# Feed-forward units moved to an earlier attention job: finer first groups of weight blocks, one converted block per job

## The chip, the cores and the metric

The kernel runs on one core of one Trainium2 chip. The metric is the device time of one execution in microseconds; less is better. The kernel before took 1116.96 us (median of three runs, 1116.5 to 1118.39).

## The reference

Two layers, one after the other. Attention with decay, 8 batches of 8 heads, 576 positions, 64 values per head:

```
scores = scale * np.matmul(q, k.transpose(0, 1, 3, 2))
log_f = np.log(np.clip(f, 0.0001, 1.0))
cum = np.cumsum(log_f, axis=-1)
decay = cum[:, :, :, None] - cum[:, :, None, :]
scores = np.where(causal, -1000000000.0, scores + decay)
...
attn = attn / (np.sum(attn, axis=-1, keepdims=True) + 1e-09)
return np.matmul(attn, v).astype(np.float32)
```

Then a feed-forward layer on the 4608 tokens of 512 values, with `w_in` of 512 x 2048 and `w_out` of 2048 x 512:

```
h = x @ w_in
g = np.where(pos, h, np.where(neg, 0.0, (h + beta) ** 2 / (4.0 * beta)))
return (g @ w_out).astype(np.float32)
```

## The kernel before

**Attention in jobs.** A job is one pair of heads of one batch. The four pairs of batch 0 are cut by rows (`CUTS`): jobs 0 to 3 do row tiles 0 and 1 (256 positions), jobs 4 to 7 tiles 2 to 4. From job 8 on a job does all five tiles (four of 128 rows, one of 64, which holds both heads) of a pair; there are 36 jobs. For a row tile, PE multiplies queries and keys into a PSUM tile `s` (`scores`, L482), of which there are two. Meanwhile POOL computes the decay scores into an `sdr` tile (L488) and masks it (L492). In `weights` DVE adds the two and takes each row's extremum in one instruction (L571, which leaves it in `nm`; below "the maximum"); ACT takes the exponential and the row sum (L575). What follows depends on the job: in jobs 0 to 4 the normalised weights are turned by PE against a diagonal (`turn_rows`: ACT makes the diagonal from the identity, L502, PE multiplies, L513, "the turning products", and ACT copies into `pT`, L524). From job 5 on they are split into two float16 halves, `pr` (ACT L589, DVE L595; for some tiles of jobs 6 and 7 POOL does the second, L593), and SP's DMA transposes them (L601, L604). The `sdr` tiles are a ring: POOL may write one again only when the job before has read it.

A job's products with the values come in the middle of the job after it (`finish`). With the last pair of a row part they make tokens of the feed-forward layer available: 256 tokens, which is chunk 0, at `finish` of job 3, that is in job 4, and 512 at `finish` of job 7.

**Weights.** The feed-forward weights are 8 blocks of 256 hidden units. A block comes as two loads (`w_in` part, `w_out` part), in words that `weight_split` turns into floats: three integer passes on DVE per load (L211, L214, L217), a sum of squares on ACT (L221), from it a scale, then a high half on ACT (L225) and a low half: on POOL for `w_in` (L227, L228), on DVE for `w_out` (L230). `CONVERT` says how many blocks are converted in which job: before, block 0 in job 1, block 1 in job 2, blocks 2 and 3 in job 3, block 4 in job 5, block 5 in job 6, the others in jobs 9 and 10.

**Feed-forward units.** A unit is one chunk of 256 tokens with one block. `moe_front` multiplies tokens and `w_in` (L657, 24 products into a tile `ph`), and ACT and DVE make the activation and its two halves `g` (L666, L667, L668, L670, L671). `moe_back`, called two units later, multiplies `g` with `w_out` (L685, 12 "output products") into a pair of PSUM tiles `po`, of which there is one pair. While not all blocks are converted, the blocks of a chunk go in groups (`EARLY`): each group has scales of its own (`moe_scales`, 17 small DVE instructions, L289 to L314), and at its end `po` is evicted: the first group of a chunk by an ACT copy into `ot` (L702), a later one by a DVE multiply and add (L698).

**The order.** `EARLY` is also the order of the first units. In each job, `ready()` counts the units whose tokens are there, and a quota of them is spread over the steps that are left in the batch. It is taken ahead of a job's steps, so job 4, in whose middle chunk 0 becomes available, has a quota of 0; jobs 5 to 8 did 2, 2, 1 and 1 units. A scheduler then sets the final order on each engine from the program; every engine works through its own list strictly in order, SP its DMA issues too.

Of the kernel before, what the change touches and what calls it, by code (L numbers as in the profile page):

```python
# [8 lines left out]
F32 = mybir.dt.float32  # L9
F16 = mybir.dt.float16  # L10
I32 = mybir.dt.int32
AF = mybir.ActivationFunctionType
ALU = mybir.AluOpType
AX = mybir.AxisListType

P = 128
EVEN_EXP = 0x7F000000
HALF_BIAS = 0x1FC00000
# [14 lines left out]

POOL_LOW = {6: (2, 4), 7: (2, 4)}

EARLY = ((0, 0, 4), (0, 4, 6), (1, 0, 4), (1, 4, 6), (0, 6, 8), (1, 6, 8))

CONVERT = {1: 1, 2: 1, 3: 2, 5: 1, 6: 1, 9: 1, 10: 2}
LOADS = {0: 3, 1: 6, 2: 8}
AHEAD = 4  # L40

# [4 lines left out]
def kernel(  # L46
# [19 lines left out]
    nc = tc.nc  # L66
# [3 lines left out]
    NPAIR = H // 2  # L70
    NT5 = -(-S // P)
# [5 lines left out]
    NB = NF // 2  # L77
# [6 lines left out]
    const = ctx.enter_context(tc.tile_pool(name="const", bufs=1))  # L84
# [3 lines left out]
    tiny = ctx.enter_context(tc.tile_pool(name="tiny", bufs=4))  # L88
# [94 lines left out]
    sw = const.tile([P, 2, NB], F32, name="sw")  # L183
# [53 lines left out]
    sv = const.tile([P, B], F32, name="sv")  # L237
# [22 lines left out]
    def value_step(b, i):  # L260

        if 0 < i <= NPAIR:
            value_max(b, i - 1)
        if i < NPAIR:
            value_load(b, i)

    def value_scale(b):
        m1 = tiny.tile([P, 1], F32, name="m1", bufs=2)
        nc.vector.tensor_reduce(out=m1, in_=vmax[b], axis=AX.X, op=ALU.max)
        m = mv[:, b:b + 1]  # L270
        across(m, m1)
        if b:
            nc.vector.tensor_tensor(out=m, in0=m, in1=mv[:, b - 1:b], op=ALU.max)
        scale_of(sv[:, b:b + 1], pv[:, b:b + 1], m)

    early_z = const.tile([P, 5, NB], F32, name="early_z")

    class Scales:
        pass

    def moe_scales(b, first=0, last=NB - 1, early_group=False):

        z = Scales()
        z.first, z.last = first, last
        blocks = slice(first, last + 1)
        n = last + 1 - first
        w = early_z[:, :, blocks] if early_group else tiny.tile([P, 5, NB], F32, name="z")
        z.t, z.h, z.u, z.r, z.o = (w[:, i] for i in range(5))
        nc.vector.tensor_scalar(out=z.t, in0=sw[:, 0, blocks], scalar1=sv[:, b:b + 1], scalar2=None, op0=ALU.mult)  # L289
        nc.vector.tensor_scalar(  # L290
            out=z.h.bitcast(I32), in0=z.t.bitcast(I32), scalar1=1, scalar2=None, op0=ALU.logical_shift_right
        )
        nc.vector.tensor_scalar(
            out=z.h.bitcast(I32), in0=z.h.bitcast(I32), scalar1=HALF_BIAS, scalar2=None, op0=ALU.add
        )
        nc.vector.reciprocal(z.u, z.h)
        nc.vector.tensor_scalar(out=z.u, in0=z.u, scalar1=0.5, scalar2=None, op0=ALU.mult)
        nc.vector.tensor_scalar(out=z.h, in0=z.h, scalar1=0.5, scalar2=None, op0=ALU.mult)
        gm = tiny.tile([P, 1], F32, name="gm", bufs=2)
        sm = tiny.tile([P, 1], F32, name="sm", bufs=2)  # L300
        nc.vector.tensor_reduce(out=gm, in_=mp[:, 0, blocks], axis=AX.X, op=ALU.max)
        nc.vector.tensor_reduce(out=sm, in_=mp[:, 1, blocks], axis=AX.X, op=ALU.max)
        nc.vector.tensor_scalar(
            out=gm, in0=gm, scalar1=mv[:, b:b + 1], scalar2=OVER * 1.001 * DM ** 0.5, op0=ALU.mult, op1=ALU.mult
        )
        nc.vector.tensor_scalar(out=gm, in0=gm, scalar1=1.0, scalar2=None, op0=ALU.max)
        even_pow2(gm, gm)
        z.osc = z.o[:, 0:1]
        nc.vector.tensor_scalar(
            out=z.osc, in0=gm, scalar1=sm, scalar2=4.0 / PSC, op0=ALU.mult, op1=ALU.mult  # L310
        )
        nc.vector.tensor_tensor(out=z.r, in0=z.t, in1=sw[:, 1, blocks], op=ALU.mult)
        nc.vector.tensor_scalar(out=z.r, in0=z.r, scalar1=z.osc, scalar2=None, op0=ALU.mult)
        nc.vector.reciprocal(z.r, z.r)  # L314
        return z
# [43 lines left out]
    def load_decay(w, h):  # L359
        bh = w.b * H + 2 * w.hp + h  # L360
        ck = two.tile([P, S], F32, name="ck", bufs=3)
        nc.sync.dma_start(
            ck[:, 0:w.s1], cum_d[bh:bh + 1, 0:w.s1].broadcast_to([P, w.s1])
        )
        w.ck.append(ck)
# [43 lines left out]
    def prepare(w):  # L409
        if w.p < NQK:  # L410
            return early_prepare(w)
        sc = w.sc
        for j in range(2):
            nc.scalar.activation(qs[:, 2 * j], w.x32[j], AF.Copy, scale=sc[:, j:j + 1])  # L414
        for j in range(2):
            nc.vector.scalar_tensor_tensor(  # L416
                out=qs[:, 2 * j + 1], in0=w.x32[j], scalar=sc[:, j:j + 1], in1=qs[:, 2 * j],
                op0=ALU.mult, op1=ALU.subtract,
            )
        qkT = two.tile([P, 4, SP], F16, name="qkT")  # L420
        nc.sync.dma_start_transpose(
            qkT.rearrange("p c (b e) -> p (c b) e", e=P), qs.rearrange("p c e -> p (c e)")
        )
        qh, ql, kh, kl = (qkT[:, c] for c in range(4))
        w.terms = ((qh, kh), (ql, kh), (qh, kl))
# [288 lines left out]

    units = [(ch, fb) for ch, first, end in EARLY for fb in range(first, end)]
    units += [(ch, fb) for ch in range(NCH) if ch not in [e[0] for e in EARLY] for fb in range(NB)]
    groups = sorted({e[1:] for e in EARLY})
    done = 0
    tokens = 0
    nload = 0  # L720
# [14 lines left out]
    def weight_step():  # L735
# [25 lines left out]
    for p in range(njobs + 1):  # L761
        w = pairs[p] if p < njobs else None
        nxt = pairs[p + 1] if p + 1 < njobs else None
        steps = []
        if w:
            if w.b not in xs:
                xs[w.b] = xpool.tile([P, NPAIR, 2, S], F16, name="x")
            if nxt:
                load_decay(nxt, 0)
                prepare(nxt)  # L770
            scores(w, w.r0)

            def step(r):
                if r + 1 < w.r1:
                    scores(w, r + 1)
                if r == w.r1 - 2 and nxt:
                    load_decay(nxt, 1)
                    split_values(nxt)
                weights(w, r)
                if r == w.r0 and p + 3 < njobs:  # L780
                    pairs.append(load(p + 3))
                if w.r1 == NT5 and w.b + 1 < B:
                    n = w.r1 - w.r0
                    i = w.hp * n + r - w.r0 - (NPAIR - 1) * n + -(-(NPAIR + 1) // n) * n
                    if 0 <= i <= NPAIR:
                        value_step(w.b + 1, i)
                    if w.hp == NPAIR - 1 and r == w.r0:
                        value_scale(w.b + 1)
                if r == w.r1 - 1 and p + 2 < njobs:
                    measure(pairs[p + 2])  # L790

            steps = [lambda r=r: step(r) for r in range(w.r0, w.r1)]
        if p > 0:
            wp = pairs[p - 1]

            def finish():
                nonlocal tokens
                (early_values if wp.p < NPE else values)(wp, xs[wp.b])
                if wp.hp == NPAIR - 1:
                    if wp.b and wp.r0 == 0:  # L800
                        join_scales(wp.b - 1)
                    tokens = wp.b * S + wp.s1

            steps.insert(4 if len(steps) == NT5 else 2, finish)
        load_weights(LOADS.get(p, 0))
        blocks = CONVERT.get(p, 0)
        quota = -(-ready() // (NPAIR - (p + NPAIR - 1) % NPAIR))
        before, converted = done, 0
        for i, st in enumerate(steps):
            st()  # L810
            while converted < blocks * (i + 1) // len(steps):
                weight_step()
                converted += 1
            while ready() and done - before < quota * (i + 1) // len(steps):
                if units[done] not in bsc and nw < 2 * NB:
                    break
                moe_unit(*units[done])
                done += 1
# [35 lines left out]
```

## Time and profile before

| | |
|---|---|
| median of three runs | 1116.96 us |
| the profiled execution | 1118.56 us |
| its span | 1116.8 us |
| mean granted PE clock | 0.966 |
| PE, DVE, ACT, POOL busy in the span | 91%, 72%, 71%, 38% |
| PE busy in 60 to 290 us | 167.05 of 230 us |
| DVE busy in 60 to 290 us | 186.47 of 230 us |

Engines: PE multiplies matrices (PEld loads its weights), DVE is the vector engine, ACT the activation engine, POOL is GpSimd, SP issues the DMAs. A row of the timeline has the start and the duration in us, the engine, the line of the kernel, the operation, what it writes and reads, a count, and in brackets how long the engine stood idle before it and whose work ended that. A group by line has count, then busy time and mean duration in ns of one, then the idle time before. The granted clock is the share of PE's full clock that it was given. In the profile's time, job 4's first maximum is at 68.21 us, job 5's at 90.88, job 6's at 111.56, job 7's at 131.19 and job 8's at 151.09.

### The profile page before, as it was taken

How to read it: one execution, taken by the hardware profiler on the slowest of the kernel's cores; microseconds unless marked ns; L12 is line 12 of the kernel's file. 1: busy time of each engine (PE TensorE's matmuls, PEld its weight loads, DVE VectorE, ACT ScalarE, POOL GpSimd, SP SyncE). 2: the span in 40 equal slices, each digit the busy share in tenths (PEclk: the TensorE clock that was granted, in tenths of full speed). 3: DMA queues.
4: the chain of work that ended last, by engine and by line, in shares of the span. 5: the costliest groups of instructions: out<-in, count | busy, mean ns of one | idle time of the engine just before them, and what ended most of it. 6: DMA issues, size and time to landing. Idle time of an engine off the chain costs nothing. (4 is left out here: it accounts for less than half of the span.)

```text
span 1116.8 us, 24410 instructions
## 1 busy us (share of the span) xinstructions
PE 1017.8 (91%) x8811; PEld 663.8 (59%) x8811; DVE 799.0 (72%) x2095; ACT 790.0 (71%) x1638; POOL 427.4 (38%) x679
## 2 busy tenths in 40 slices
PE   4647789667999999999999999999999999999998
PEld 3424455335566666666766666566666666677665
DVE  4785987887989888887667668888888787322222
ACT  3665887756877887788667768787878887444443
POOL 3486665634544543343223324344343442000000
PEclk9968889778999999999999999999999999999999
DMA  7957765575978657766653666775776462200000
GB/s 235 303 143 222 167 147 125 142 191 116 190 172 166 159 143 170 167 152 148 118 140 78 155 119 153 168 174 139 166 167 155 116 124 73 66 21 1 19 20 19
DMA packets 408281, 152.18 MB, mean 136 GB/s; under 512 B 383968, under 2 KB 384992, under 8 KB 408160
## 3 DMA queue, kind: packets, MB, share of 16 engines
q1 hardware_dynamic: 408160, 150.63, 57.6%
q8 instruction: 69, 1.13, 0.4%
q14 instruction: 52, 0.43, 0.1%
HBM read 75.64 MB, written 9.58 MB: 76 GB/s over the span
## 5 line engine op out<-in xcount | busy, mean ns | idle before, releaser
L657 PE MATMUL ph<-x,place 128*128 128x256 f16 (+3 forms) x4608 | 413.3, 248 | 6.4 <-DVE u L668 5.5
L685 PE MATMUL po<-place,g 128*128 128x512 f16 x1728 | 401.9, 382 | 12.4 <-ACT g L670 8.2
L657 PEld LDWEIGHTS <-place 128*128 128x128 f16 x4608 | 354.1, 99 | 66.3 <-issue 18.0
L685 PEld LDWEIGHTS <-g 128*128 128x128 f16 x1728 | 166.4, 99 | 192.0 <-ACT g L670 10.5
L488 POOL TENSOR_SCALAR sdr<-ck,nsig,cqs 128x128 f32<-128x128 f32 (+1 forms) x192 | 145.8, 763 | 149.2 <-DVE pr L595 137.3
L575 ACT ACTIVATE sdr<-sdr,nm 128x384 f32<-128x384 f32 (+1 forms) x248 | 137.4, 554 | 66.9 <-DVE nm L571 57.0
L668 DVE SCALAR_TENSOR_TENSOR u<-ph,z,u 128x512 f32<-128x512 f32 x128 | 95.8, 748 | 113.1 <-ACT u L667 112.5
L488 POOL TENSOR_SCALAR sd<-ck,nsig,cqs 64x576 f32<-64x576 f32 x48 | 60.0, 1250 | 248.7 <-ACT qs L414 109.3
L666 ACT ACTIVATE u<-ph,z 128x512 f32<-128x512 f32 x128 | 97.9, 765 | 78.4 <-PE ph L657 78.4
L482 PE MATMUL s<-qkT 64*64 64x512 f16 (+11 forms) x1056 | 119.6, 342 | 34.1 <-DVE nm L571 30.6
L595 DVE SCALAR_TENSOR_TENSOR pr<-sdr,rc,pr 128x384 f16<-128x384 f32 (+2 forms) x232 | 130.5, 596 | 21.6 <-ACT pr L589 20.4
L670 ACT ACTIVATE g<-u,z 128x512 f16<-128x512 f32 x128 | 91.9, 718 | 67.6 <-DVE u L668 67.3
L671 DVE SCALAR_TENSOR_TENSOR g<-u,z,g 128x512 f16<-128x512 f32 x128 | 96.7, 756 | 47.2 <-ACT g L670 46.5
L589 ACT ACTIVATE pr<-sdr,rc 128x384 f16<-128x384 f32 (+1 forms) x236 | 119.3, 556 | 12.1 <-DVE rc L586 5.3
L571 DVE CUSTOM_DVE_ANT_0 sdr<-s,sdr,nalpha 128x128 f32<-128x128 f32 (+1 forms) x192 | 99.0, 545 | 13.1 <-PE s L482 8.3
L492 POOL TENSOR_SCALAR_AFFINE_SELECT sdr<-sdr 128x128 f32<-128x128 f32 x248 | 93.9, 389 | 9.7
L667 ACT ACTIVATE u<-u 128x512 f32<-128x512 f32 x144 | 89.5, 622 | 2.0
L615 PE MATMUL s<-pT,vs 128*64 128x320 f16 (+3 forms) x1098 | 70.9, 282 | 4.7 <-DVE nm L571 4.7
L615 PEld LDWEIGHTS <-vs 128*64 128x64 f16 x1098 | 49.7, 112 | 27.3 <-issue 8.8
L488 POOL TENSOR_SCALAR sdr<-ck,cq 128x384 f32<-128x384 f32 (+3 forms) x56 | 39.9, 712 | 66.2 <-DVE pr L595 38.3
L482 PEld LDWEIGHTS <-qkT 64*128 64x128 f16 (+1 forms) x864 | 33.8, 99 | 51.3 <-issue 35.9
L414 ACT ACTIVATE qs<-qk,sc 128x640 f16<-128x640 f32 x48 | 37.0, 818 | 22.4 <-DVE sc L140 22.4
(154 smaller groups left out, 1013.8 us busy)
## 6 DMA issues: line engine op xcount, KB each, us to landing
ck<-cum_d SPq DMA_DIRECT2D x64, 288.0 KB, 3.8
out_dram<-ot SPq DMA_DIRECT2D x36, 256.0 KB, 2.1
qk<-in_k_dram SPq DMA_DIRECT2D x64, 128.0 KB, 2.7
vst<-in_v_dram SPq DMA_DIRECT2D x28, 288.0 KB, 3.3
v<-in_v_dram SPq DMA_DIRECT2D x62, 128.0 KB, 2.6
qk<-in_q_dram SPq DMA_DIRECT2D x56, 128.0 KB, 2.7
place<-in_moe_w_in_dram SPq DMA_DIRECT2D x6, 1024.0 KB, 7.2
place<-in_moe_w_out_dram SPq DMA_DIRECT2D x5, 1024.0 KB, 7.2
```

What stands on the lines that cost most here:

```text
L482: nc.tensor.matmul(sds[h % len(sds)][1][p0:p1, c0:c1], lhsT=a[rows, q0 - w.s0:q0 - w.s0 + p1 - p0], rhs=b[rows, c0:c1], start=(i == 0), st ...
L488: nc.gpsimd.tensor_scalar(out=sd[p0:p1, 0:wid], in0=w.ck[h][p0:p1, 0:wid], scalar1=w.nsig if w.p < NQK else w.nsig[p0:p1], scalar2=w.cqs[p ...
L571: nc.vector.tensor_tensor_reduce(out=a, in0=sp[:, 0:wid], in1=a, scale=w.nalpha, scalar=BIG, op0=ALU.add, op1=ALU.min, accum_out=nm[:, i:i ...
L575: nc.scalar.activation(a, a, AF.Exp, bias=nm[:, i:i + 1], scale=-1.0, accum_out=sm[:, i:i + 1])
L589: nc.scalar.activation(pr[:, :, 0, i, :], a, AF.Copy, scale=rc[:, i:i + 1])
L595: nc.vector.scalar_tensor_tensor(out=pr[:, :, 1, i, :], in0=a, scalar=rc[:, i:i + 1], in1=pr[:, :, 0, i, :], op0=ALU.mult, op1=ALU.subtract,)
L615: nc.tensor.matmul(av[64 * h:64 * h + 64, at + s0:at + s1], lhsT=w.vs[:, vl, h, t, :], rhs=w.pT[:, t, pl, h, s0:s1], start=(t == 0 and pi ...
L657: nc.tensor.matmul(ph[:, fi, a0:a1], lhsT=wi[fb][:, wl, t, fi * P:(fi + 1) * P], rhs=xs[b][:, t, xl, s0:s0 + a1 - a0], start=(fi == 0 and ...
L666: nc.scalar.activation(u, h, AF.Relu, scale=z.u[:, i:i + 1], bias=z.h[:, i:i + 1])
L668: nc.vector.scalar_tensor_tensor(out=u, in0=h, scalar=z.t[:, i:i + 1], in1=u, op0=ALU.max, op1=ALU.min)
L671: nc.vector.scalar_tensor_tensor(out=g[:, 1], in0=u, scalar=z.r[:, i:i + 1], in1=g[:, 0], op0=ALU.mult, op1=ALU.subtract)
L685: nc.tensor.matmul(po[ch][i], lhsT=g[:, gl, fi * TC + i * P:fi * TC + (i + 1) * P], rhs=wo[fb][:, wl, fi, :], start=(first and fi == 0 and ...
```

## The change

Chunk 0's first six blocks go in three groups of two; chunk 1's first six in one. Job 4 is put into a new table `FIRST`: `finish` comes ahead of its row tiles instead of among them, and directly behind it two units are done, (0, 0) and (0, 1); jobs 5 to 8 then have one each. Block 3 is converted in job 4 instead of job 3, so jobs 1 to 6 convert one block each. As groups now overlap (blocks 0 to 5 as one group for chunk 1, as three for chunk 0), the part of the scales that depends on a block alone is computed once for each block (`block_scales`), and each group has its own place for the rest.

```diff
-EARLY = ((0, 0, 4), (0, 4, 6), (1, 0, 4), (1, 4, 6), (0, 6, 8), (1, 6, 8))
+EARLY = ((0, 0, 2), (0, 2, 4), (0, 4, 6), (1, 0, 6), (0, 6, 8), (1, 6, 8))
+FIRST = {4: 2}
-CONVERT = {1: 1, 2: 1, 3: 2, 5: 1, 6: 1, 9: 1, 10: 2}
+CONVERT = {1: 1, 2: 1, 3: 1, 4: 1, 5: 1, 6: 1, 9: 1, 10: 2}
...
+        if early_group:
+            at = groups.index((first, last + 1))
+            z.t, z.h, z.u = (early_z[:, i * NB + first:i * NB + first + n] for i in range(3))
+            z.r = early_r[:, starts[at]:starts[at] + n]
+            z.osc = early_r[:, starts[-1] + at:starts[-1] + at + 1]
+            fresh = slice(made[0], last + 1)
+            if made[0] <= last:
+                block_scales(*(early_z[:, i * NB + made[0]:i * NB + last + 1] for i in range(3)), b, fresh)
+                made[0] = last + 1
...
-            steps.insert(4 if len(steps) == NT5 else 2, finish)
+            steps.insert(0 if p in FIRST else 4 if len(steps) == NT5 else 2, finish)
...
-        quota = -(-ready() // (NPAIR - (p + NPAIR - 1) % NPAIR))
+        quota = FIRST.get(p) or -(-ready() // (NPAIR - (p + NPAIR - 1) % NPAIR))
...
-            while ready() and done - before < quota * (i + 1) // len(steps):
+            while ready() and done - before < (quota if p in FIRST else quota * (i + 1) // len(steps)):
```

What this moves on three engines, as the order of the instructions has it (each row is one instruction, or several alike with their count; the line numbers of after are higher by 19 in most of the rows shown, and by 1 in `weight_split`).

POOL, before, between the last tile of job 4 and the first of job 5. `place` is the weight store, `ck` and `cq` are the decay sums; `sdr_101` and `sdr_102` are the scores of job 5's first tile, one for each head:

```order
L488 TENSOR_SCALAR sd_1_106<-ck,cq 64x576
L492 AFFINE_SELECT sd_1_106<-sd_1_106 64x64
L227 TENSOR_SCALAR place<-place,sw 128x1024
L228 TENSOR_TENSOR place<-place 128x1024
L227 TENSOR_SCALAR place<-place,sw 128x1024
L228 TENSOR_TENSOR place<-place 128x1024
L488 TENSOR_SCALAR sdr_101<-ck,cq 128x384
L488 TENSOR_SCALAR sdr_102<-ck,cq 128x384
```

And after:

```order
L228 TENSOR_SCALAR place<-place,sw 128x1024
L511 AFFINE_SELECT sd_1_106<-sd_1_106 64x64
L507 TENSOR_SCALAR sd_1_106<-ck,cq 64x576
L229 TENSOR_TENSOR place<-place 128x1024
L511 AFFINE_SELECT sd_1_106<-sd_1_106 64x64
L507 TENSOR_SCALAR sdr_101<-ck,cq 128x384
L507 TENSOR_SCALAR sdr_102<-ck,cq 128x384
```

Before, blocks 2 and 3 stand ahead of job 5's scores; after, block 2 alone.

PE, before, from the transposes of job 5's queries and keys to job 4's turning products (L513):

```order
L388 MATMUL s<-ident,qk_0_98 128x128 x4
L388 MATMUL s<-ident,qk_0_98 128x64
L131 MATMUL ph<-m2w,ones 128x2
L482 MATMUL s<-qkT 128x384 x2
L513 MATMUL ph<-pr_112,sdr_101 128x128 x2
L513 MATMUL ph<-pr_112,sdr_102 128x128
```

After, from the scores of job 4's last tile on; the 48 front products of the two units (L676) stand ahead of these rows:

```order
L501 MATMUL s<-qkT 64x512 x2
L501 MATMUL s<-qkT 64x64 x2
L407 MATMUL s<-ident,qk_0_98 128x128 x2
L407 MATMUL s<-ident,qk_0_98 128x64
L407 MATMUL s<-ident,qk_0_98 128x128 x4
L407 MATMUL s<-ident,qk_0_98 128x64
L501 MATMUL s<-qkT 128x384 x2
L704 LDWEIGHTS g
L704 MATMUL po_1012<-place,g 128x512
```

With the last row begin 16 output products; the turning products (L532 now) come behind them, and eight more output products ahead of the second tile's.

POOL, before, at job 8's first tile (`sdr_101` and `sdr_102` are its two heads, `pr` and `sd` belong to job 7):

```order
L488 TENSOR_SCALAR sdr_101<-ck,cq 128x128
L227 TENSOR_SCALAR place<-place,sw 128x1024
L492 AFFINE_SELECT sdr_101<-sdr_101 128x128
L593 TENSOR_TENSOR pr_1276<-sdr_102,pr_1276 128x3x128
L228 TENSOR_TENSOR place<-place 128x1024
L488 TENSOR_SCALAR sdr_102<-ck,cq 128x128
L593 TENSOR_TENSOR pr_1381<-sd_1_106,pr_1381 128x5x128
L492 AFFINE_SELECT sdr_102<-sdr_102 128x128
```

And after:

```order
L612 TENSOR_TENSOR pr_1308<-sdr_102,pr_1308 128x3x128
L507 TENSOR_SCALAR sdr_101<-ck,cq 128x128
L507 TENSOR_SCALAR sdr_102<-ck,cq 128x128
L511 AFFINE_SELECT sdr_101<-sdr_101 128x128
L511 AFFINE_SELECT sdr_102<-sdr_102 128x128
L228 TENSOR_SCALAR place<-place,sw 128x1024
L229 TENSOR_TENSOR place<-place 128x1024
```

Both heads now stand ahead of the weight block's two instructions.

More of the change, by code (lines that the diff above doesn't have):

```diff
@@ L274, in value_scale, with block_scales @@
         scale_of(sv[:, b:b + 1], pv[:, b:b + 1], m)
-    early_z = const.tile([P, 5, NB], F32, name="early_z")
+    groups = sorted({e[1:] for e in EARLY})
+    starts = [sum(e - f for f, e in groups[:i]) for i in range(len(groups) + 1)]
+    early_z = const.tile([P, 3 * NB + starts[-1] + len(groups)], F32, name="early_z")
+    early_r = early_z[:, 3 * NB:]
+    made = [0]
     class Scales:
         pass
+    def block_scales(t, h, u, b, blocks):
+        nc.vector.tensor_scalar(out=t, in0=sw[:, 0, blocks], scalar1=sv[:, b:b + 1], scalar2=None, op0=ALU.mult)
+        nc.vector.tensor_scalar(
+            out=h.bitcast(I32), in0=t.bitcast(I32), scalar1=1, scalar2=None, op0=ALU.logical_shift_right
+        )
+        nc.vector.tensor_scalar(
+            out=h.bitcast(I32), in0=h.bitcast(I32), scalar1=HALF_BIAS, scalar2=None, op0=ALU.add
+        )
+        nc.vector.reciprocal(u, h)
+        nc.vector.tensor_scalar(out=u, in0=u, scalar1=0.5, scalar2=None, op0=ALU.mult)
+        nc.vector.tensor_scalar(out=h, in0=h, scalar1=0.5, scalar2=None, op0=ALU.mult)
     def moe_scales(b, first=0, last=NB - 1, early_group=False):
@@ L286, in moe_scales @@
         n = last + 1 - first
[L287 to L298, printed above, removed]
+        if early_group:
[7 more added lines that the diff above has]
+                made[0] = last + 1
+        else:
+            w = tiny.tile([P, 5, NB], F32, name="z")
+            z.t, z.h, z.u, z.r = (w[:, i] for i in range(4))
+            z.osc = w[:, 4, 0:1]
+            block_scales(z.t, z.h, z.u, b, blocks)
         gm = tiny.tile([P, 1], F32, name="gm", bufs=2)
@@ L307, in moe_scales @@
         even_pow2(gm, gm)
-        z.osc = z.o[:, 0:1]
         nc.vector.tensor_scalar(
@@ L716 @@
     units += [(ch, fb) for ch in range(NCH) if ch not in [e[0] for e in EARLY] for fb in range(NB)]
-    groups = sorted({e[1:] for e in EARLY})
     done = 0
```

## Prediction

> **What bounds the kernel now.** I read the busy time by stretches first: the start, the stretch in which attention and feed-forward units are mixed but PE is not full, the full stretch, and the tail.
>
> ```profile
> 0.00:60.00 60.00, 35.46 (x152) 24.15 (x154) 36.36 (x93) 33.10 (x86) 25.23 (x53) 1.00 0.87 264
> 60.00:290.00 230.00, 167.05 (x1116) 99.30 (x1112) 186.47 (x504) 164.29 (x339) 135.78 (x178) 0.84 0.66 157
> 290.00:960.00 670.00, 662.30 (x6301) 435.94 (x6300) 533.30 (x1443) 527.55 (x1121) 266.39 (x450) 1.00 0.66 146
> 960.00:1117.00 157.00, 153.03 (x1250) 104.36 (x1248) 42.83 (x57) 65.06 (x93) 0.00 (x0) 1.00 0.04 14
> ```
>
> The columns are the stretch, its length, busy time of PE, PE weight loads, DVE, ACT and POOL, the granted clock, the DMA share and GB/s. From 290 us on PE is busy for 815 of 827 us: there the time is its work, which the change doesn't alter. In 60 to 290 PE idles 63 us and DVE, the fullest engine, 44. The change lies in jobs 3 to 8, in this stretch. As the same six units are done when job 8 ends, what counts is how much earlier the attention jobs pass through it; that shift goes to the end at full value.
>
> Next, the same columns close around the moved work:
>
> ```profile
> 63.00:70.00 7.00, 0.38 (x2) 0.30 (x2) 7.00 (x11) 3.06 (x7) 6.84 (x6) 0.71 0.75 189
> 70.00:76.00 6.00, 0.00 (x0) 0.00 (x0) 3.45 (x7) 3.77 (x6) 5.55 (x7) 0.50 0.11 29
> 76.00:82.00 6.00, 4.54 (x17) 2.21 (x17) 5.36 (x14) 4.43 (x12) 5.50 (x7) 0.50 0.31 73
> ...
> 162.00:170.00 8.00, 8.00 (x67) 4.29 (x64) 5.86 (x18) 7.52 (x17) 4.05 (x10) 1.00 0.26 78
> ```
>
> ```profile
> 120.00:140.00 20.00, 16.28 (x136) 10.50 (x132) 18.91 (x31) 15.95 (x30) 16.78 (x17) 0.99 0.68 144
> ```
>
> From 63 to 82 POOL is the full engine (17.9 of 19 us), PE nearly empty at half clock, ACT idle for 7.7 us. From 120 to 140 DVE is full. So job 4 waits for POOL's decay scores, and jobs 6 and 7 for DVE.
>
> **The change part by part.** First POOL and DVE in jobs 4 to 6 (start, length, engine, line):
>
> ```profile
> 64.80 2.38 POOL L492 TENSOR_SCALAR_AFFINE_SELECT sdr<-sdr 128x128 f32<-128x128 f32 x2
> 67.15 2.71 POOL L228 TENSOR_TENSOR place<-place 128x1024 f16<-128x1024 f32 x1
> 71.15 2.62 POOL L488 TENSOR_SCALAR sdr<-ck,cq 128x384 f32<-128x384 f32 x2
> 84.81 1.18 POOL L227 TENSOR_SCALAR place<-place,sw 128x1024 f32<-128x1024 f32 x1 [1.79 <-ACT place L225]
> 86.07 3.02 POOL L228 TENSOR_TENSOR place<-place 128x1024 f16<-128x1024 f32 x1
> 89.20 1.28 POOL L488 TENSOR_SCALAR sdr<-ck,cq 128x384 f32<-128x384 f32 x2
> 90.55 0.54 POOL L492 TENSOR_SCALAR_AFFINE_SELECT sdr<-sdr 128x128 f32<-128x128 f32 x2
> 91.19 1.48 POOL L488 TENSOR_SCALAR sdr<-ck,cq 128x512 f32<-128x512 f32 x2
> ```
>
> ```profile
> 75.84 0.56 DVE L571 CUSTOM_DVE_ANT_0 sdr<-s,sdr 128x384 f32<-128x384 f32 x1 [2.55 <-POOL sdr L492]
> 83.38 0.14 DVE L301 TENSOR_REDUCE gm<-mp 128x1 f32<-128x4 f32 x1
> 84.81 0.18 DVE L314 RECIPROCAL early_z<-early_z 128x4 f32<-128x4 f32 x1
> 90.88 0.56 DVE L571 CUSTOM_DVE_ANT_0 sdr<-s,sdr 128x384 f32<-128x384 f32 x1 [3.76 <-POOL sdr L492]
> 109.03 0.75 DVE L256 TENSOR_REDUCE m<-vst 128x1 f32<-128x576 f32 x1 [3.01 <-DMA vst<-in_v_dram]
> 109.70 0.68 DVE L211 TENSOR_SCALAR qs<-place 128x1024 int32<-128x1024 int32 x1
> 111.56 0.55 DVE L571 CUSTOM_DVE_ANT_0 sdr<-s,sdr 128x384 f32<-128x384 f32 x1
> ```
>
> *Term 1, job 4's first tiles.* Block 3's integer steps leave DVE between 62 and 78, where they run beside POOL. POOL's instructions there are slow: two selects in 2.38 us against 0.54 at 90.55, a pair of decay scores in 2.62 against (1.28 + 1.48) / 2 = 1.38. Undisturbed, these and the subtraction (2.71, against 2.10 for the same one at 151.90, quoted in term 5) give 1.84 + 1.24 + 0.6 = 3.7 us, so the row maximum at 75.84 comes up to 3.7 us earlier. But the two units now stand here. Their pieces, in a grouping by line of 60 to 290 us (busy, mean ns):
>
> ```profile
> L666 ACT ACTIVATE u<-ph,early_z 128x512 f32<-128x512 f32 x15 | 11.4, 769 | 3.4 <-PE ph L657 3.4
> L668 DVE SCALAR_TENSOR_TENSOR u<-ph,early_z,u 128x512 f32<-128x512 f32 x15 | 11.1, 743 | 0.2 <-ACT u L667 0.2
> L671 DVE SCALAR_TENSOR_TENSOR g<-u,early_z,g 128x512 f16<-128x512 f32 x15 | 11.0, 745 | 0.2
> L225 ACT ACTIVATE place<-place,sw 128x1024 f16<-128x1024 f32 x9 | 10.6, 1213 | 2.2 <-DVE sw L140 2.2
> L670 ACT ACTIVATE g<-u,early_z 128x512 f16<-128x512 f32 x15 | 10.5, 713 | 3.8 <-DVE u L668 3.8
> L667 ACT ACTIVATE u<-u 128x512 f32<-128x512 f32 x15 | 9.2, 617 | 0.0
> ```
>
> A unit costs ACT 0.77 + 0.62 + 0.71 = 2.1 us and DVE 1.5. Two cost ACT 4.2, ahead of the diagonals that open job 4's turning products. ACT's 7.7 idle us hold them, but in order with the exponentials, so the 3.7 gained are used up: term 1 is 0 (between -3.7 and +0.5).
>
> *Term 2, PE.* The two units' 48 front products fall into PE's gap and cost nothing. Their output products don't: 16 of the 24 stand ahead of job 4's turning products, whose source tiles POOL must overwrite for job 5.
>
> ```profile
> 76.46 2.19 PE L482 MATMUL s<-qkT 64*64 64x512 f32 x8 [12.24 <-DVE nm L571]
> 84.01 2.73 PE L513 MATMUL ph<-pr,sdr 128*128 128x128 f32 x12
> 91.98 1.19 PE L482 MATMUL s<-qkT 64*64 64x512 f32 x8 [2.19 <-DVE nm L571]
> 104.92 1.04 PE L685 MATMUL po<-place,g 128*128 128x512 f16 x4 [0.16 <-ACT g L670]
> ```
>
> At 104.92 one takes 0.26 us, so 16 take 4.2; the turning products end at 90.9 instead of 86.7. Block 3's POOL part (1.79 wait, 1.18, 3.02), which held POOL until 89.20, is gone from here, so POOL waits for PE: job 5's first scores at 90.9 instead of 89.20, +1.7. The bounds are 0 (the products start earlier) and, with a product at half clock, 0.52 us as the pair 76.46 and 91.98 shows (2.19 against 1.19), 8.3 us: +5.8. I take +1.7, since two units' fronts have just woken the clock.
>
> The trace shows the clock at 0.50 after a 12 us gap. The Trainium skill, "TensorE: Matmul & The Clock Gate", Part 1, says that an idle window of about 3.4 us throttles PE and some 3.4 us of work releases it. By that rule an idle gap while ACT copies job 5's transposes would cost about 1.7 us more here, and the sum would be near -1.0 instead of -2.7.
>
> *Term 3, job 5.* Out of it: DVE's wait for a value load (3.0), block 4's first steps, which stood ahead of job 6's first maximum (109.70 to 111.56, 1.9), and one unit's ACT work (2.1). Into it: block 3's two scaled copies on ACT (2.4), ahead of the copies that job 5's third tile waits for, and the new eviction of the first pair, two ACT copies:
>
> ```profile
> L702 ACT ACTIVATE ot<-po,early_z x4: 667/670/675, 165.7 to 236.0; 128x512 f32<-128x512 f32 x4
> ```
>
> of 0.67, so 1.35; and small scale steps, in DVE's idle time. -7.0 + 3.75 = -3.2; with term 2 job 6's first maximum comes at about 110.0.
>
> *Term 4, jobs 6 and 7, DVE full.* The 1.9 us of block 4 are owed; a unit's 1.5 is paid already. The change has 29 more DVE instructions, for two more groups. A group's 17, from 83.38 to 84.99, take 1.6 us, 0.095 each, 2.7 in all; half of it in full stretches, 1.4. Sum +1.8. The unit that leaves job 6 takes its ACT work along too, beside a full DVE: nothing.
>
> *Term 5, job 8.* Now POOL's halving of block 5 stands between the two heads of job 8's first tile, and PE waits:
>
> ```profile
> 148.62 1.20 POOL L227 TENSOR_SCALAR place<-place,sw 128x1024 f32<-128x1024 f32 x1
> 151.90 2.10 POOL L228 TENSOR_TENSOR place<-place 128x1024 f16<-128x1024 f32 x1
> ```
>
> ```profile
> 151.09 0.29 DVE L571 CUSTOM_DVE_ANT_0 sdr<-s,sdr 128x128 f32<-128x128 f32 x1
> 156.89 0.28 DVE L571 CUSTOM_DVE_ANT_0 sdr<-s,sdr 128x128 f32<-128x128 f32 x1
> ```
>
> ```profile
> 155.44 1.65 PE L482 MATMUL s<-qkT 64*128 64x384 f32 x4 [3.49 <-DVE nm L571]
> ```
>
> Both heads now come ahead of it. 1.20 + 2.10 = 3.3 us go from the second maximum, against 3.49 that PE waits; I take -3.0. The bounds are 0, as PE is full from 162 on, and -4.5, most of the 5.8 between the heads.
>
> Evictions balance: four for chunk 0 and two for chunk 1, against three and three. SP's queue gets the later weight loads behind job 5's transposes; the blocks they feed are converted a job or two later, so nothing is charged.
>
> Sum: 0 + 1.7 - 3.2 + 1.8 - 3.0 = -2.7 us. The profiled execution took 1118.56 (span 1116.8, 1.8 around it), so 1115.9; it lies 1.6 above the median 1116.96, from which the forecast is 1114.3.
>
> **The rivals.** *No change*: term 5 falls away, because PE's units fill 162 to 170 (8.00 of 8) and job 9 waits for them anyway. Then +0.3, 1117.3. For it speaks that row, against it the 3.49 us that PE stands idle before.
>
> *Slower*: the output products run at half clock behind ACT's long chain and hold POOL: term 2 is +5.8, and the eight others, ahead of the second tile's turning products, add 8 x 0.26 = 2.1. The sum is -2.7 + 4.1 + 2.1 = +3.5, 1120.5. For it: the clock of 0.50 in 70 to 82. Against it: 48 products just before. It decides if job 4's last 128-row turning products end after about 98 us.
>
> *Larger gain*: the fronts keep the clock up through the gap. PE's 4.54 us in 76 to 82, at 0.50, halve (-2.3) and term 2 goes to 0 (-1.7). The sum is -2.7 - 2.3 - 1.7 = -6.7, 1110.3. Against it: ACT, not PE, sets the pace there.
>
> That the change doesn't do what it says is excluded by the order: the fronts do stand in job 4.
>
> **How the numbers follow.** Forecast 0.40, larger gain 0.14, no change 0.22, slower 0.24. A difference of 0.2%, 2.2 us, is about what a measurement of this kernel can tell from none. The forecast lies half a microsecond beyond that, so I give three quarters of it to faster: 0.30 + 0.14 = 0.44; same 0.10 + 0.22 = 0.32; slower 0.24. The bounds of terms 2 and 5 carry the forecast from 1111 to 1121.4; the larger gain, with half of term 1's 3.7 kept as well, reaches 1108.5. Range 1108.5 to 1121.5.
>
> **What would show it.** Job 5's first maximum near 92.5, job 6's near 110, job 8's two first maxima within 1.5 us, PE's clock above 0.7 in 70 to 76 and its full stretch beginning some 3 us sooner. The prediction is wrong if job 6's first maximum is later than 112, if job 8's heads are still 4 us apart, or if the shift at job 8 doesn't reach the end.

## The result and the profile after

The changed kernel takes 1132.53 us (median of four runs, 1130.58 to 1133.86) against 1117.68 for the kernel before in the same comparison (1116.5 to 1118.69): a ratio of 1.0132, 95% interval 1.0111 to 1.0153. It is 15 us slower, where 2.7 us faster was forecast, and outside the range. The profiled execution of the changed kernel took 1133.58 us with a span of 1131.8. Its line numbers are 19 higher behind `moe_scales`: the maximum is L590 now, the turning products L532, the output products L704, and in `weight_split` one higher (squares L222, scaled copies L226, POOL's halving L228 and L229, DVE's L231). Of the scale steps, L288 to L297 are those of a block (`block_scales`), L321 to L333 those of a group.

The same stretches as before, changed kernel (columns as in the prediction):

```profile
60.00:290.00 230.00, 169.47 (x1063) 98.48 (x1063) 187.27 (x510) 157.55 (x325) 124.94 (x168) 0.82 0.65 152
290.00:960.00 670.00, 656.16 (x6240) 430.45 (x6239) 532.55 (x1447) 526.69 (x1124) 272.08 (x461) 1.00 0.72 145
63.00:70.00 7.00, 4.89 (x43) 3.72 (x44) 7.00 (x18) 3.78 (x8) 6.71 (x8) 1.00 0.87 206
70.00:76.00 6.00, 3.60 (x28) 2.20 (x26) 3.61 (x10) 5.47 (x11) 5.47 (x9) 0.98 0.45 107
76.00:82.00 6.00, 5.06 (x15) 2.21 (x16) 5.97 (x14) 4.31 (x12) 3.32 (x4) 0.50 0.85 263
120.00:140.00 20.00, 15.36 (x91) 9.85 (x89) 17.65 (x34) 12.06 (x23) 10.49 (x11) 0.57 0.69 153
162.00:170.00 8.00, 5.99 (x45) 3.77 (x43) 7.57 (x26) 4.06 (x12) 5.26 (x7) 1.00 0.45 146
```

The units fill PE's gap in 63 to 76, as planned. But 120 to 140 is poorer on every engine, PE at a clock of 0.57, and PE, which was full in 162 to 170, now idles a quarter of it. From 290 on, where before PE was all but full, it is busy for 656.16 of 670 us against 662.30.

Where the time went is read from the maxima on DVE. Changed kernel: job 4 (second head), 5, 6, 7, job 8's two heads, job 8's second tile, job 9, job 15:

```profile
73.20 0.56 DVE L590 CUSTOM_DVE_ANT_0 sdr<-s,sdr 128x384 f32<-128x384 f32 x1 [2.36 <-POOL sdr L511]
89.06 0.56 DVE L590 CUSTOM_DVE_ANT_0 sdr<-s,sdr 128x384 f32<-128x384 f32 x1 [0.85 <-POOL sdr L511]
109.28 0.56 DVE L590 CUSTOM_DVE_ANT_0 sdr<-s,sdr 128x384 f32<-128x384 f32 x1 [0.97 <-PE s L501]
132.06 0.54 DVE L590 CUSTOM_DVE_ANT_0 sdr<-s,sdr 128x384 f32<-128x384 f32 x1
149.84 0.29 DVE L590 CUSTOM_DVE_ANT_0 sdr<-s,sdr 128x128 f32<-128x128 f32 x1 [0.94 <-POOL place L228]
150.06 0.29 DVE L590 CUSTOM_DVE_ANT_0 sdr<-s,sdr 128x128 f32<-128x128 f32 x1
165.13 0.41 DVE L590 CUSTOM_DVE_ANT_0 sdr<-s,sdr 128x256 f32<-128x256 f32 x1
184.32 0.29 DVE L590 CUSTOM_DVE_ANT_0 sdr<-s,sdr 128x128 f32<-128x128 f32 x1 [0.24 <-PE s L501]
355.68 0.35 DVE L590 CUSTOM_DVE_ANT_0 sdr<-s,sdr,nalpha 128x128 f32<-128x128 f32 x1
```

Of the kernel before, the three that the prediction didn't show (job 8's second tile, job 9, job 15):

```profile
154.62 0.41 DVE L571 CUSTOM_DVE_ANT_0 sdr<-s,sdr 128x256 f32<-128x256 f32 x1
177.51 0.29 DVE L571 CUSTOM_DVE_ANT_0 sdr<-s,sdr 128x128 f32<-128x128 f32 x1 [1.37 <-PE s L482]
345.19 0.35 DVE L571 CUSTOM_DVE_ANT_0 sdr<-s,sdr,nalpha 128x128 f32<-128x128 f32 x1
```

Up to job 6 the changed kernel is 2.3 us ahead (109.28 against 111.56). At job 7 it is 0.9 behind, and job 8's two heads come together, 1.2 and 6.8 us earlier. Then the second tile of that same job is 10.5 us late. Job 9 is 6.8 late, job 15 10.5, the end 15.

What stands between the heads and the second tile of job 8, in the timelines of ACT, POOL, PE and DVE of the changed kernel:

```profile
151.94 1.11 ACT L222 ACTIVATE place<-place 128x1024 f16<-128x1024 f32 x1 [5.02 <-POOL place L229]
```

```profile
148.55 1.16 POOL L228 TENSOR_SCALAR place<-place,sw 128x1024 f32<-128x1024 f32 x1
149.80 2.11 POOL L229 TENSOR_TENSOR place<-place 128x1024 f16<-128x1024 f32 x1
...
157.68 1.40 POOL L612 TENSOR_TENSOR pr<-sd,pr 128x640 f16<-128x640 f32 x1 [4.01 <-ACT sd L611]
159.07 1.18 POOL L228 TENSOR_SCALAR place<-place,sw 128x1024 f32<-128x1024 f32 x1
```

```profile
154.30 0.59 PE L132 MATMUL ph<-m2w,ones 128*128 128x2 f32 x2 [4.61 <-ACT place L222]
```

```profile
154.92 0.16 DVE L133 TENSOR_SCALAR mp<-ph 128x2 f32<-128x2 f32 x1 [4.57 <-PE ph L132]
...
156.14 0.14 DVE L321 TENSOR_REDUCE gm<-mp 128x1 f32<-128x6 f32 x1
...
157.72 1.39 DVE L296 TENSOR_SCALAR early_z<-early_z 128x2 f32<-128x2 f32 x1
...
159.09 1.32 DVE L332 TENSOR_SCALAR early_z<-early_z 128x6 f32<-128x6 f32 x2
160.33 0.28 DVE L333 RECIPROCAL early_z<-early_z 128x6 f32<-128x6 f32 x2
...
160.72 1.45 DVE L231 SCALAR_TENSOR_TENSOR place<-x,sw,place 128x1024 f16<-128x1024 f32 x1
162.15 2.39 DVE L614 SCALAR_TENSOR_TENSOR pr<-sdr,rc,pr 128x128 f16<-128x128 f32 x2
```

This reads as a chain. ACT's sum of squares of block 5 (L222) writes its unneeded element results into a `place` that still holds block 4's raw words. POOL reads these for block 4's low half (148.55 to 151.91), and on POOL that now stands behind job 8's scores. So ACT stands still for 5.02 us, with all its later work in line behind. PE's norm product waits 4.61 for ACT, DVE's next step 4.57 for PE. On DVE the rest of block 5 then stands ahead of the second tile's maximum: the scale steps of two groups that end with this block, (4, 5) and (0 to 5), from 156.14 to 160.61, its low half (1.45), and the products L614.

The kernel before has the same wait, but a short one:

```profile
138.02 1.17 ACT L221 ACTIVATE place<-place 128x1024 f16<-128x1024 f32 x1 [1.14 <-POOL place L228]
```

There POOL began block 4's low half at 134.24, 14.3 us earlier than the 148.55 of the changed kernel. Two waits for loads lie ahead of that in the changed kernel. DVE begins block 4's first pass at 117.46, directly behind the first of the two rows below, where the kernel before began it at 109.70. And POOL stands still for decay rows just ahead of job 8's scores:

```profile
116.79 0.75 DVE L257 TENSOR_REDUCE m<-vst 128x1 f32<-128x576 f32 x1 [3.94 <-DMA vst<-in_v_dram]
```

```profile
142.49 0.75 POOL L507 TENSOR_SCALAR sd<-ck,cq 64x576 f32<-64x576 f32 x1 [5.73 <-DMA ck<-cum_d]
```

No run was made to take these two waits away, so what they are worth is open.

### The profile page after: what moved, and what is told of

The parts are those of the page before. It is cut to its first block, busy times and chain, and to the rows that moved or that the text cites. A ratio compares the mean times of both kernels' runs of the same rounds, so it can differ in the third digit from the quotient of the medians.

```text
span 1131.8 us, 24413 instructions
## 1 busy us (share of the span) xinstructions
PE 1028.0 (91%) x8811; PEld 666.7 (59%) x8811; DVE 807.4 (71%) x2119; ACT 791.2 (70%) x1638; POOL 419.5 (37%) x679
## 5 line engine op out<-in xcount | busy, mean ns | idle before, releaser
L676 PE MATMUL ph<-x,place 128*128 128x256 f16 (+3 forms) x4608 | 417.2, 250 | 10.3 <-DVE u L687 8.3
L704 PE MATMUL po<-place,g 128*128 128x512 f16 x1728 | 402.0, 382 | 7.6 <-ACT g L689 4.3
L676 PEld LDWEIGHTS <-place 128*128 128x128 f16 x4608 | 355.6, 99 | 70.9 <-issue 17.7
L704 PEld LDWEIGHTS <-g 128*128 128x128 f16 x1728 | 166.2, 99 | 187.7 <-issue 8.1
L614 DVE SCALAR_TENSOR_TENSOR pr<-sdr,rc,pr 128x384 f16<-128x384 f32 (+2 forms) x232 | 130.6, 597 | 20.7 <-ACT pr L608 19.6
L590 DVE CUSTOM_DVE_ANT_0 sdr<-s,sdr,nalpha 128x128 f32<-128x128 f32 (+1 forms) x192 | 98.9, 544 | 11.2 <-PE s L501 6.3
L511 POOL TENSOR_SCALAR_AFFINE_SELECT sdr<-sdr 128x128 f32<-128x128 f32 x248 | 87.6, 365 | 9.6
L634 PE MATMUL s<-pT,vs 128*64 128x320 f16 (+2 forms) x1098 | 72.5, 285 | 6.8 <-DMA pT<-pr 6.0
```

Of the source, the lines that this page charges most:

```text
L590: nc.vector.tensor_tensor_reduce(out=a, in0=sp[:, 0:wid], in1=a, scale=w.nalpha, scalar=BIG, op0=ALU.add, op1=ALU.min, accum_out=nm[:, i:i ...
L614: nc.vector.scalar_tensor_tensor(out=pr[:, :, 1, i, :], in0=a, scalar=rc[:, i:i + 1], in1=pr[:, :, 0, i, :], op0=ALU.mult, op1=ALU.subtract,)
L634: nc.tensor.matmul(av[64 * h:64 * h + 64, at + s0:at + s1], lhsT=w.vs[:, vl, h, t, :], rhs=w.pT[:, t, pl, h, s0:s1], start=(t == 0 and pi ...
L676: nc.tensor.matmul(ph[:, fi, a0:a1], lhsT=wi[fb][:, wl, t, fi * P:(fi + 1) * P], rhs=xs[b][:, t, xl, s0:s0 + a1 - a0], start=(fi == 0 and ...
L704: nc.tensor.matmul(po[ch][i], lhsT=g[:, gl, fi * TC + i * P:fi * TC + (i + 1) * P], rhs=wo[fb][:, wl, fi, :], start=(first and fi == 0 and ...
```

## The experiments

**One part undone, one part alone.** The change has three parts that can be put back apart: the groups (`EARLY`), the units in front (`FIRST`), the conversions (`CONVERT`). Theory A is the chain just shown, set off by the conversions. Theory B blames the units in front, theory C the groups. All runs are compared by their ratio to the kernel before, which ran beside each (its median went from 1116.28 to 1119.55 over the comparisons).

```diff
-CONVERT = {1: 1, 2: 1, 3: 1, 4: 1, 5: 1, 6: 1, 9: 1, 10: 2}
+CONVERT = {1: 1, 2: 1, 3: 2, 5: 1, 6: 1, 9: 1, 10: 2}
```

> The changed kernel with the conversions of the kernel before (two blocks in job 3, none in job 4). Theory A (block 3 in job 4 pushes block 4's low half behind job 8's first scores on POOL, ACT waits 5.0 us for it with block 5's squares, job 8's second tile is 10 us late): the 5.0 us wait is gone and the time falls to 1114 to 1121. Theory B (the two units in front of job 4: cold clock, late turning products): stays at 1128 to 1134. Theory C (more scale groups on DVE, other order of units): stays at 1127 to 1133.

Measured: 1132.19 us, ratio 1.0137 (1.0108 to 1.0166). As slow as the changed kernel, although ACT's wait for POOL is down to 2.5 us. Theory A isn't the whole cause.

```diff
-FIRST = {4: 2}
+FIRST = {}
```

> The changed kernel without the two units and the finish in front of job 4; groups and conversions as changed. Theory A: 1127 to 1134, and ACT still waits for POOL's subtraction of block 4 before block 5's squares unless the order on POOL turns by itself. Theory B: 1114 to 1120. Theory C: 1127 to 1133.

Measured: 1127.43 us, 1.0090 (1.0063 to 1.0118), and ACT's wait is there (4.7 us). Against theory B: without the front the kernel is some 5 us faster (0.42%, plus or minus 0.35), and its order is another one.

The conversions alone (`EARLY` as before and `FIRST = {}`):

> The kernel before with the conversions alone changed (one block in each of jobs 1 to 6). Theory A: 1126 to 1133, slower than before by 0.8% or more. Theory B: 1115 to 1120. Theory C: 1115 to 1120.

Measured: 1124.78 us, 1.0071 (1.0047 to 1.0095), under theory A's range and over that of B and C. The view of waits from 100 to 172 us has theory A's wait:

```profile
ACT place L222 <- POOL place L229: 4.8, 1, 4.8
```

The units in front alone (`EARLY` and `CONVERT` as before), then the groups alone (`FIRST = {}`, `CONVERT` as before):

> The kernel before with the two units and the finish in front of job 4 alone. Theory B (the units themselves cost: their output products and ACT work stand ahead of job 4's softmax, so job 5 starts late, as in the run with conversions as before, where job 5's first maximum was at 95.94): 1125 to 1132, job 5's first maximum at 94 to 97. If the grouping and not the front is what costs in that run: 1115 to 1119.

> The kernel before with the groups of blocks (two, two, two; six) alone changed. Theory B: 1117 to 1120, the cost of 29 more small DVE steps and one eviction more. If the grouping costs by its order of units: 1122 to 1130.

Measured: 1125.81 us, 1.0060 (1.0037 to 1.0084), and 1124.43 us, 1.0047 (1.0031 to 1.0064). The front alone does what theory B says: POOL waits for the turning products, and job 5's first maximum is at 96.81, where the changed kernel has 89.06.

```profile
95.14 1.27 POOL L507 TENSOR_SCALAR sdr<-ck,cq 128x384 f32<-128x384 f32 x2 [5.34 <-PE ph L532]
```

```profile
96.81 0.56 DVE L590 CUSTOM_DVE_ANT_0 sdr<-s,sdr 128x384 f32<-128x384 f32 x1 [2.91 <-POOL sdr L511]
```

But each part alone costs 5 to 8 us and the three together 15. Front and groups together cost as much as all three, groups and conversions 10; front and conversions weren't run. No single part is the cause.

**The chain by itself.** Theory A's wait can be taken away by other data places, with the order of PE, ACT, DVE and POOL the same (in SP's queue block 4's two loads change places). With block 4's halves swapped, block 5's squares write where DVE has read, long before.

```diff
-RAW = (2, 4, 6, 8, 10, 12, 14, "early", 10, 12, 14, "next", "early", 14, "early", "early")
+RAW = (2, 4, 6, 8, 10, 12, 14, "early", 12, 10, 14, "next", "early", 14, "early", "early")
```

> The changed kernel with the raw words of block 4's two halves in each other's place, so that block 5's squares write into a place that DVE has read out, not POOL; nothing else is changed. Theory A: ACT's 5.0 us wait for POOL's subtraction is gone, job 8's second tile comes 4 to 6 us sooner and the time falls by 4 to 6 us to 1126 to 1129. If the loads that stand in SP's queue ahead of the transposes set the pace (theory D: POOL waits 9.4 and 5.7 us for its decay rows, DVE 6.3 for value loads), the wait goes too but the time falls by under 1.5 us: 1131 to 1133.

Measured: 1127.99 us, 1.0094 (1.0065 to 1.0122). Since this interval touches that of the changed kernel, the two ran once more side by side:

> The changed kernel once more, beside the next run. Ratio to the kernel before as in the result, 1.011 to 1.0155; reference for the next.

> The changed kernel with the raw places of block 4 swapped, order the same. Theory A: 2.5 to 5 us under the run beside it. If the wait was hidden and the first difference the chip's: within 1.5 us of it.

Measured: 1132.07 us, 1.0123 (1.0107 to 1.0140), and 1128.81 us, 1.0089 (1.0072 to 1.0106): 3.3 us. First the changed kernel, then the swapped one: ACT's squares of block 5 and the maximum of job 8's second tile.

```profile
151.81 1.11 ACT L222 ACTIVATE place<-place 128x1024 f16<-128x1024 f32 x1 [5.38 <-POOL place L229]
...
164.99 0.41 DVE L590 CUSTOM_DVE_ANT_0 sdr<-s,sdr 128x256 f32<-128x256 f32 x1
```

```profile
145.00 1.15 ACT L222 ACTIVATE place<-place 128x1024 f16<-128x1024 f32 x1
...
160.33 0.40 DVE L590 CUSTOM_DVE_ANT_0 sdr<-s,sdr 128x256 f32<-128x256 f32 x1
```

The wait is gone and the second tile is 4.7 us earlier. Of these, 1.3 are there at job 7's first maximum already (130.26 against 131.57), ahead of the wait. In the first pair the second tile is at 162.36 against 165.13, with job 7's at 132.30 against 132.06. So the wait is worth 3.0 to 3.4 us at job 8, and the medians have 3.3 at the end. This part of the cause is shown: 3.3 of 15 us. It is the most that can be put down to the wait, as the swap also takes away what the kernel before has of it.

**Loads in SP's queue.** In the changed kernel two loads stand in SP's queue ahead of job 5's second transpose, which takes 6.79 us; before, they were out at 87.14 and 89.12. Changed kernel, SP:

```profile
104.21 0.37 SPq L202 DMA_DIRECT2D x<-in_moe_w_in_dram  x1
...
105.46 0.54 SPq L202 DMA_DIRECT2D place<-in_moe_w_in_dram  x1
...
106.65 6.79 SPq L620 DMA_TRANSPOSE pT<-pr  x1
```

Theory L: the first of them, block 6's, needed only in job 9, is what delays the transposes and all behind. One small DVE copy makes it wait for block 4's scale:

```diff
+        if n == 12:
+            nc.vector.tensor_copy(out=early[0:1, 0:1], in_=sw[0:1, 0, 4:5])
```

> The changed kernel, with one small DVE copy of block 4's scale into the buffer of block 6's first half ahead of its load, so that this load (not needed before job 9) leaves SP's queue ahead of job 5's transposes and follows job 6's. Theory L (loads in the queue: the two loads at 104.21 and 105.46 share the DMA engines with job 5's transposes, the second of which takes 6.79 us, and push value loads and decay rows behind): the transposes take 3 us less, job 7's first maximum comes 2 to 4 us sooner than 132.06, the time falls by 2 to 4 us to 1128.5 to 1130.5. Theory A (block 5's squares wait for POOL's reading of block 4) alone: within 1 us of 1132.5.

> The swap of the raw places and the later load of block 6 together. If A and L add: 4.5 plus 2 to 4 us under the changed kernel, 1124 to 1126. If the one only uncovers the other: 1127 to 1129, as with the swap alone.

> The kernel before with the later load of block 6 (28 rows on ACT move). Theory L: there too the load stands in front of job 5's transposes, 1 to 3 us faster, 1114 to 1116. Theory R with few rows moved: within 1.5 us of before.

Measured: 1127.46 us, 1.0074 (1.0058 to 1.0090); with the swap 1124.11 us, 1.0050 (1.0031 to 1.0069), again 3.3 us less, in nearly the same order (ACT's is the same, DVE's differs in 22 of 2120 rows, POOL's in 3 of 679); and on the kernel before 1121.30 us, 1.0025 (1.0009 to 1.0041), slower, not faster. There ACT's wait for POOL is 3.38 us instead of 1.14. The gain is there, but not as theory L has it: job 7's first maximum came at 136.26, 4 us later than in the changed kernel. The edit had also made the scheduler write a new order for jobs 6 to 14 on all engines. So theory R: the new order made the gain. Two edits separate bytes and order: half of the load's bytes in nearly the old order (half of these weights are left out), and a quarter loaded twice, with a new order.

```diff
-        nc.sync.dma_start(raw(n).rearrange("p (t c) -> p t c", t=src.shape[1]), src)
+        dst = raw(n).rearrange("p (t c) -> p t c", t=src.shape[1])
+        part = 2 if n == 12 else src.shape[1]
+        nc.sync.dma_start(dst[:, 0:part], src[:, 0:part])
```

> The changed kernel with only half the bytes of block 6's first load (the other half of those weights is left out); the order of the instructions stays almost word for word (8 of 1243 rows on ACT). Theory L (the bytes themselves, in front of job 5's transposes): the load lands in 5.8 us, half of that is 2.9, so the time falls by 1.5 to 3 us to 1129.5 to 1131. Theory R (the run with the later load gained because the scheduler wrote a new order for jobs 6 to 14 with it, 249 rows on ACT, not because of the bytes): within 1 us of 1132.5.

```diff
+        if n == 12:
+            nc.sync.dma_start(dst[:, 0:1], src[:, 0:1])
```

> The changed kernel with a quarter of block 6's first load loaded a second time (256 KB more); the scheduler writes a new order for jobs 6 to 14 (308 rows on ACT). Theory L: 0.7 to 1.5 us slower, 1133 to 1134. Theory R: the new order decides, so the time leaves the changed kernel's by 2 us or more, either way: 1124 to 1130 or 1135 to 1140.

Measured: 1133.35 us, 1.0124 (1.0108 to 1.0141), with half the bytes; 1126.50 us, 1.0065 (1.0048 to 1.0081), with more bytes than before. As far as the bytes of this load go, theory L falls: taking half of them away did nothing, and the transpose even took longer, as the SP row of the run with half the load shows:

```profile
107.06 7.93 SPq L622 DMA_TRANSPOSE pT<-pr  x1
```

Adding a useless quarter saved some 7 us (0.67%): more bytes are no reason for that, and the order is what else changed. ACT's wait for POOL is still there in that run (5.87 us); the better order gains between jobs 11 and 12 (job 12's first maximum is at 269.25, in the changed kernel at 275.69), not in job 8. An edit to the second of the two loads, block 5's, was not tried.

**How far an order moves the time.** Three more kernels with orders of their own:

> The conversions alone changed, with the raw places of block 4 swapped. Theory A (that kernel waits 4.8 us on ACT for POOL's reading of block 4): 3 to 4 us under that kernel's ratio of 1.0071, so 1.003 to 1.0045, 1120 to 1122. Theory R: the scheduler writes a new order here too (173 rows on ACT), so 2 us or more off that range either way.

> The changed kernel with the raw places swapped and a quarter of block 6's load made twice. Theory A adds 3 us to the gain of the second load's order: 1121 to 1124. Theory R: the scheduler writes yet another order (162 rows on ACT against the run with the second load alone), so 2 us or more off that range, either way.

> Groups and conversions as changed, no units in front of job 4, raw places swapped, block 6's load later. Theory B (the front costs 4 to 5 us): 1117 to 1121, the 4.6 us over before that the same kernel with the front had are gone. Theory R: 1120 to 1128, with no sign of the front.

Measured: 1122.20 us, 1.0026 (1.0009 to 1.0042); 1127.89 us, 1.0086 (1.0069 to 1.0104); 1124.45 us, 1.0057 (1.0038 to 1.0076). The first is 0.45% under the conversions alone (1.0071), a little more than theory A says, but its order is another one too, so wait and order can't be told apart in it. In the second the wait for POOL is gone as well, yet it isn't faster than the same kernel with that wait in another order (1.0065). The third has no units in front and isn't faster than the same kernel with them (1.0050): under these orders the front's cost doesn't show.

Last, both kernels with the order made by the scheduler's other mode:

```diff
-    with tile.TileContext(nc, schedule_with_timeline_sim=True) as tc:
+    with tile.TileContext(nc, schedule_with_timeline_sim=False) as tc:
```

> The kernel before with the scheduler's timeline mode off, so that all engines get another order. Reference for the next run; the order of the kernel before is one that came out well, so by theory R this is slower by 5 to 40 us: 1122 to 1160.

> The changed kernel with the scheduler's timeline mode off. If the 12 us are the change's own (the units in front, the groups, 29 more DVE steps): 8 to 15 us above the run with the kernel before in this mode. Theory R (the change itself is worth what was forecast, and the order made the loss): from 5 us under it to 3 us above it.

Measured: 1201.34 us, 1.0753 (1.0714 to 1.0793), and 1197.67 us, 1.0725 (1.0696 to 1.0755). The mode costs more than expected, 83 us. But in it the changed kernel is 3.7 us ahead by the medians; the intervals overlap, so a gain isn't shown, but a loss of 8 to 15 us is excluded in this mode (the difference is -0.28%, plus or minus 0.5). So the change doesn't cost 15 us in every order. That it costs nothing in an order as good as that of the kernel before isn't shown: in this mode PE is far from full behind 290 us (busy for 613.67 and 612.25 of 670 us up to 960), so a late job could be hidden there, and ACT's wait for POOL is 3.9 us in the kernel before and 2.6 in the changed one.

No version beat the kernel before. The best were 0.25% behind (its own load later, and the conversions alone with swapped places); the best with the whole change was 0.50% behind.

## Why the prediction was wrong, point by point

**Term 1, job 4's first tiles: better than taken.** The second head came 2.6 us earlier (75.84 to 73.20); I had given all of it to ACT's work for the units.

**Term 2, PE: the wait came, its price didn't.** POOL does wait for the turning products now, and the 16 output products ahead of them take 5.08 us, 0.32 each where 0.26 was taken, part of them at half clock:

```profile
79.67 5.08 PE L704 MATMUL po<-place,g 128*128 128x512 f16 x16
84.58 1.50 PE L532 MATMUL ph<-pr,sdr 128*128 128x128 f32 x12
```

```profile
86.03 2.63 POOL L507 TENSOR_SCALAR sdr<-ck,cq 128x384 f32<-128x384 f32 x2 [6.46 <-PE ph L532]
```

But the sum put these products behind the times of the kernel before, and what stands ahead of them on PE came earlier too: job 5's first scores at 77.99 where they were at 82.42. So the turning products end at 86.08 and not at 90.9, and POOL starts job 5 at 86.03, 3.2 us earlier than before (89.20), where 1.7 later was forecast. Job 5's first maximum was at 89.06 and not near 92.5.

**Terms 3 and 4: the places came near, by luck.** Job 6's first maximum was at 109.28 (forecast near 110), job 7's at 132.06 (131.19 - 1.5 + 1.8 = 131.5). But from job 5 to job 6 the changed kernel won 0.5 us, where term 3 has 3.2; the error of term 2 made up for it. From job 6 to job 7 it lost 3.2 us, where term 4 has 1.8. Term 3 left out block 3's low half on DVE:

```profile
101.17 3.01 DVE L231 SCALAR_TENSOR_TENSOR place<-x,sw,place 128x1024 f16<-128x1024 f32 x1
```

And the wait for a value load, which it took out, only went behind job 6's first maximum: it is the 3.94 us at 116.79, and in 100 to 172 DVE waits 6.3 us for value loads against the 3.0 of before. One count was wrong as well: a group has 15 scale steps, not 17, and the change 24 more DVE instructions, not 29 (2119 against 2095), which moves the 2.7 us of term 4 by 0.1.

**Term 5 is the step that failed.** The prediction put it so: "Both heads now come ahead of it. 1.20 + 2.10 = 3.3 us go from the second maximum, against 3.49 that PE waits; I take -3.0." The heads did come so, to the row. But POOL's work that went behind them is not free. I followed it on POOL and not to the engine that waits for its place: the runs showed ACT standing 5.0 us there, worth 3.3 at the end. I also followed job 8 only to its first tile: the scale steps for which I took 1.4 us stand in one piece, 4.5 us long, ahead of the second (two of the rows there are long beside POOL's; see the last section). The second tile was 10.5 us late where I had the job 3 us early.

**The sum's premise failed with it.** What was to go "to the end at full value" was applied to a shift at one row. The order from job 8 to job 14 was written anew too, and I priced one place of it. From job 9 (6.8 us late) to job 15 (10.5) the changed kernel lost 3.7 us more, and 4.5 on the way to the end, where the prediction has PE full and nothing lost. About 2.9 of these go between 438 and 468 us, where DVE stands behind value loads that arrive late; changed kernel:

```profile
453.76 0.75 DVE L257 TENSOR_REDUCE m<-vst 128x1 f32<-128x576 f32 x1 [2.39 <-DMA vst<-in_v_dram]
458.45 0.75 DVE L257 TENSOR_REDUCE m<-vst 128x1 f32<-128x576 f32 x1 [1.42 <-DMA vst<-in_v_dram]
```

That this loss belongs to the order isn't shown. In the other profiled execution of the changed kernel (`changed_beside`) the same two waits are 1.47 and 0.43 us, and from job 15 to the end it lost 1.4 us, not 4.5.

**The queue on SP, "so nothing is charged":** not refuted, but not shown either. The loads came to stand between job 5's two transposes (100.49 and 106.65), not behind both. Halving one of them didn't shorten the time, and the other wasn't tried.

**The rivals:** none had a place behind job 8. The slower one, output products at half clock that hold POOL, happened in part (0.50 in 76 to 82, the wait of 6.46) and cost nothing at job 5 in the changed kernel. Its sign didn't come: job 4's last 128-row turning products ended at 92.06 and not after 98. With the front alone it did cost, 5.9 us at job 5.

**What stays open:** of the 15 us, 3.3 are the place wait, by runs in the same order. Some 5 to 7 go with other orders of jobs 6 to 14, and which rows of the order carry them wasn't separated. With the swap and the order of the later load together, 5.6 us are left (1.0050), whose cause isn't shown. Candidates that no run separated are the waits for the value load at 116.79 and for the decay rows at 142.49. The low clock in 120 to 140 wasn't followed; over whole executions it doesn't go with the time: the four of the changed kernel took 1130.58, 1131.48, 1133.58 and 1133.86 us at a mean clock of 0.947, 0.951, 0.962 and 0.962.

## What to carry to other kernels

Where a scheduler writes the order, an edit changes more than it says: here orders for nearly the same work lay some 7 us apart, and none tried with the change came up to the kernel before. Before a suspect is charged, test it with an edit that leaves the order of all engines as it was (other places, fewer bytes), and compare the orders to be sure. And when work moves behind something, follow its buffers, not only its engine: who writes next into the place that it still reads, and what stands in line behind that writer.

## What the runs showed of the hardware

DVE steps on 2 and 6 numbers a row took 1.39 and 1.32 us (the rows at 157.72 and 159.09, of which the second is two steps), where such steps take about 0.15, as the one between the two does:

```profile
159.02 0.15 DVE L297 TENSOR_SCALAR early_z<-early_z 128x2 f32<-128x2 f32 x1
```

They lie beside POOL's rows at 157.68 (1.40) and 159.07 (1.18), start just behind them, and end with them to within 0.2 us. The Trainium skill, "SBUF — State Buffer", section "SBUF: two separate sides", says that GpSimd shares a port pair with DVE (for DVE's 2-port modes, or two inputs in SBUF) as an exclusive lock: the one that comes first holds it for its whole instruction, and the other blocks. The trace agrees, with these numbers; which mode these steps ran in, it doesn't show. So a small DVE step beside POOL can cost what is left of POOL's instruction, and not the 0.1 us at which I had priced it.

The clock fell to 0.50 without a long gap. Between 67.79 and 75.80 PE's longest gap is 1.98 us, and in the 3.4 us ahead of the fall PE was busy for 1.76 (the last two rows have the columns of the tables by stretch):

```profile
69.26 2.58 PE L676 MATMUL ph<-x,place 128*128 128x256 f16 x22 [1.47 <-POOL place L229]
73.82 1.19 PE L501 MATMUL s<-qkT 64*64 64x512 f32 x8 [1.98 <-DVE nm L590]
```

```profile
72.40:75.80 3.40, 1.76 (x11) 0.81 (x11) 2.60 (x5) 3.40 (x7) 3.15 (x6) 1.00 0.41 100
75.80:79.20 3.40, 2.26 (x9) 1.32 (x9) 3.40 (x5) 2.56 (x7) 3.22 (x3) 0.50 0.65 181
```

The Trainium skill, "TensorE: Matmul & The Clock Gate", Part 1, puts the fall after an idle window of about 3.4 us. Here no stretch of that length is idle, and the measured fall decides.
